# A first feed-forward stage computed as seven block products instead of eight

## The chip, the cores and the metric

The kernel runs on one core of one Trainium2 chip. The metric is the device time of one execution in microseconds, the median of three runs. The engines are called PE (TensorE; PEld is its weight load), DVE (VectorE), ACT (ScalarE), POOL (GpSimd) and SP (SyncE, which here only issues DMAs).

## The reference

```python
# q, k, v: (4, 12, 448, 64) float32; w1, w2, w3, w_out: 768x768; w_in: 768x2048; w_out2: 2048x768
scores = q @ k.transpose(0, 1, 3, 2) / sqrt(64) - log(448)
attn = (1 / (1 + exp(-scores))) @ v                      # a sigmoid, no softmax
x = attn.transpose(0, 2, 1, 3).reshape(1792, 768)
h = maximum(maximum(x @ w1, x @ w2), x @ w3)             # stage b below
y = h @ w_out                                            # stage c
d = y @ w_in                                             # stage d
g = maximum(d, 0) + alpha * minimum(d, 0)
out = g @ w_out2                                         # stage e
```

The weights come as 64-bit floats, all else as 32-bit floats.

## The kernel before

Every matmul has 32-bit operands in a reduced format (fp32r), so each operand is split into a high part `hi` (a cast on ACT) and the rest `lo` (a subtraction on DVE), and a product is three matmuls: lo x hi, hi x lo, hi x hi. Activations are kept transposed: 128 features on the partitions, tokens in the columns. Weights are the stationary operand, loaded in units of 768 rows by 128 columns as two halves of 384; a half arrives as pairs of 32-bit words, ACT and DVE rebuild a 32-bit float of it (`first`, `unit`, `shift`, `sign`, `whole_word`), and then `hi` and `lo` split it. Three raw buffers (`wr`) hold halves; `load_half(z + 3)` is issued on SP's queue behind `whole_word` of half z.

**Attention** works on 24 pairs of heads, two pairs an iteration. For each pair SP loads q and k by 128-byte runs into three buffers each, POOL loads v; DVE turns q and k, casts and subtracts (`prep_ops`); PE computes scores by chunks of 128 keys into three PSUM buffers of two banks (`scores`), one sigmoid on ACT reads 896 columns, and `av` multiplies by v into `pav`. `to_x` casts and subtracts `pav` straight into the x tiles. The 1792 tokens are cut in tiles of 512, 512, 512 and 256, so a batch of 448 straddles two tiles. From pair 12 on, operations that convert the first two weight units are slipped in (`early`).

**Stage b** (`ff1`) takes for each of the six blocks of 128 features of h the units of w1, w2, w3, and for each unit the four token tiles: 6 row blocks x 3 matmuls of 512 columns, or for the short tile 12 matmuls of 512 and 256 with hi and lo side by side. The first result is copied to `mx`, the others are maximized into it on DVE; the third is split into h, which stays in SBUF. **Stage c** is the same over h. **Stages d and e** (`ff2`) alternate in eight steps of two units of w_in (d) and two rows of w_out2 (e); e's sums are kept in SBUF and added to on DVE; the short tile of e swaps its operands (`e_short`).

Nothing is scheduled by a tool: the order of each engine is the order of the program. Conversion work waits in a list (`pending`), of which a fixed number of operations is run after each PSUM group.

Of the kernel before, what the change touches and what calls it, by code (L numbers as in the profile page):

```python
# [16 lines left out]
P = 128  # L17


@with_exitstack  # L20
def kernel(
# [14 lines left out]

# [22 lines left out]
    assert KH == P // 2 and 2 * D == P and (H // 2) % 2 == 0  # L59
# [5 lines left out]
    UN = 768  # L65
    HF = UN // 2
    T = B * S
    TW = 512
    spans = [(c, min(TW, T - c)) for c in range(0, T, TW)]
    NT = len(spans)  # L70
    HW = spans[-1][1]
    assert 2 * HW == TW
# [5 lines left out]
    tpool = ctx.enter_context(tc.tile_pool(name="tpool", bufs=1))  # L78
    xpool = ctx.enter_context(tc.tile_pool(name="xpool", bufs=1))
# [7 lines left out]
    units = []  # L87
    for m in range(KF1):
        for w in (w1, w2, w3):
            units.append((w, "col", m, "w"))  # L90
    for m in range(KDM):
        units.append((w_o1, "col", m, "w"))
    SK = 2
    for s in range(KF2 // SK):
        for f in range(SK):
            units.append((w_in, "col", SK * s + f, "w"))
        for f in range(SK):
            units.append((w_o2, "row", SK * s + f, "e"))
    NU = len(units)

    epool = {}
    wraw, wsp = {}, {}

    def load_half(z):
        u, h = divmod(z, 2)
        if u >= NU:
            return
        w, kind, m, _ = units[u]
        t = wpool.tile([P, HF, 2], U32, tag="wr", name=f"wr{z}", bufs=3)
        if kind == "col":  # L110
            nk = HF // P
            nc.sync.dma_start(
                out=t.rearrange("p (k f) t -> p k (f t)", k=nk),
                in_=w[h * nk * P : (h + 1) * nk * P, 2 * m * P : 2 * (m + 1) * P].rearrange(
                    "(k p) f -> p k f", p=P
                ),
            )
        else:
            nc.sync.dma_start(
                out=t.rearrange("p f t -> p (f t)"),  # L120
                in_=w[m * P : (m + 1) * P, 2 * h * HF : 2 * (h + 1) * HF],
            )
        wraw[z] = t

    def conv_ops(u):

        if u >= NU:
            return []
        tag = units[u][3]
        ops = []  # L130

        def begin():
            pool = epool["e"] if tag == "e" else wpool
            wsp[u] = (
                pool.tile([P, UN], F32R, tag=f"{tag}h", name=f"wh{u}", bufs=2),
                pool.tile([P, UN], F32R, tag=f"{tag}l", name=f"wl{u}", bufs=2),
            )

        for h in range(2):
            z = 2 * u + h  # L140
            st = {}

            def part(i, u=u, h=h):

                if units[u][1] == "col":
                    return wsp[u][i][:, h * HF : (h + 1) * HF]
                return wsp[u][i].rearrange("p (m g j) -> p g m j", m=KDM, g=4)[:, 2 * h : 2 * h + 2]

            def seen(x, u=u):
                x = x.bitcast(F32)  # L150
                return x if units[u][1] == "col" else x.rearrange("p (g m j) -> p g m j", g=2, m=KDM)

            def first(z=z, h=h, st=st):
                if h == 0:
                    begin()
                st["r"] = wraw.pop(z)
                st["T"] = wpool.tile([P, HF], U32, tag="wt", name=f"wt{z}", bufs=3)
                nc.scalar.activation(  # L158
                    st["T"].bitcast(F32),
                    st["r"][:, :, 1].bitcast(F32),  # L160
                    AF.Abs,
                    scale=2.0**-112,
                )

            def unit(st=st):
                nc.scalar.activation(st["r"][:, :, 0], st["r"][:, :, 0], AF.Copy, scale=2.0**-29)  # L166

            def shift(st=st):
                nc.vector.tensor_scalar(st["T"], st["T"], 3, None, ALU.logical_shift_left)

            def sign(st=st):
                nc.vector.scalar_tensor_tensor(  # L172
                    out=st["r"][:, :, 0],
                    in0=st["r"][:, :, 1],
                    scalar=0x80000000,
                    in1=st["r"][:, :, 0],
                    op0=ALU.bitwise_and,
                    op1=ALU.bitwise_or,
                )

            def whole_word(z=z, st=st):
                nc.vector.tensor_tensor(out=st["T"], in0=st["r"][:, :, 0], in1=st["T"], op=ALU.add)  # L182
                load_half(z + 3)

            def hi(st=st, part=part, seen=seen):
                nc.scalar.copy(part(0), seen(st["T"]))  # L186

            def lo(st=st, part=part, seen=seen):
                nc.vector.tensor_sub(part(1), seen(st["T"]), part(0).bitcast(F32))  # L189

            ops += [first, unit, shift, sign, whole_word, hi, lo]
        return ops

    def tmp(nm, t):
        return tpool.tile([P, TW], F32, tag="tmp", name=nm, bufs=5)[:, : spans[t][1]]


    def three(x):
        return x[:, 0], x[:, 1], x.rearrange("p a n -> p (a n)")

    def xy_tile(nm, t):
        if t == NT - 1:
            x = xpool.tile([P, KDM, 2, HW], F32R, tag=f"xyh{t}", name=f"{nm}{t}")
            return [three(x[:, r]) for r in range(KDM)]
        h = xpool.tile([P, KDM, TW], F32R, tag=f"xyh{t}", name=f"{nm}h{t}")
        l = xpool.tile([P, KDM, TW], F32R, tag=f"xyl{t}", name=f"{nm}l{t}")
        return [(h[:, r], l[:, r], None) for r in range(KDM)]


    def attention(apool, ps_s, ps_v):  # L210
# [4 lines left out]
        pairs = [(b, p) for b in range(B) for p in range(NPAIR)]  # L215
# [6 lines left out]
        def load_first():  # L222

            kn = apool.tile([P, NB32, 32], F32, tag="kr", name="kn", bufs=3)
            qn = apool.tile([P, NB32, 32], F32, tag="qr", name="qn", bufs=3)
            for t, src, queue in ((kn, k, nc.sync), (qn, q, nc.scalar)):
                queue.dma_start(
                    out=t.rearrange("p n d -> p (n d)"),
                    in_=src[0, :2].rearrange("j (p n) d -> (j p) (n d)", p=D),
                )  # L230
            raw[0] = (qn, kn)

        def first_pair():

            qn, kn = raw.pop(0)
            for which, t in (("k", kn), ("q", qn)):
# [14 lines left out]
                else:  # L251
                    hi = apool.tile([P, S], F32R, tag="qh", name="qh0", bufs=2)
                    lo = apool.tile([P, S], F32R, tag="ql", name="ql0", bufs=2)
# [22 lines left out]
        def load_pair(i):  # L276
# [3 lines left out]
            qr = apool.tile([P, NB32, 32], F32, tag="qr", name=f"qr{i}", bufs=3)  # L280
            kr = apool.tile([P, NB32, 32], F32, tag="kr", name=f"kr{i}", bufs=3)
# [12 lines left out]
        def prep_ops(i):  # L294
# [6 lines left out]
            def turn(which, src):  # L301
                t = apool.tile([P, S], F32, tag=f"{which}t", name=f"{which}t{i}", bufs=2)
# [9 lines left out]
            def cut(which, copy=nc.vector.tensor_copy):  # L312
# [4 lines left out]
                else:  # L317
                    hi = apool.tile([P, S], F32R, tag="qh", name=f"qh{i}", bufs=2)
                    lo = apool.tile([P, S], F32R, tag="ql", name=f"ql{i}", bufs=2)
# [12 lines left out]
        def scores(i, c, sc=None, stop=True):  # L332
# [20 lines left out]
            if stop:  # L353
                key = (i // 2, "s") if c == NCH else (i, c)
                a = apool.tile([P, 2, S], F32, tag="a", name=f"a{i}_{c}", bufs=2 * NCH + 1)
                at[key] = a
                nc.scalar.activation(a, sc[:, :, :S], AF.Sigmoid, bias=bias_s, scale=scale)  # L357
            return sc

        def av(i, c, start, stop):  # L360
# [5 lines left out]
            for j in range(2):  # L366
# [3 lines left out]
                    a[r, j, :],  # L370
# [17 lines left out]
        def to_x(i):  # L388
            b, p = pairs[i]
            pav = pv.pop(i)  # L390
            parts = []
            for t, (c0, w) in enumerate(spans):
                c, e = max(c0, b * S), min(c0 + w, b * S + S)
                if c < e:
                    if t not in xt:
                        xt[t] = xy_tile("x", t)
                    xh, xl, _ = xt[t][p]
                    parts.append((xh[:, c - c0 : e - c0], xl[:, c - c0 : e - c0], pav[:, c - b * S : e - b * S]))
            for xh, _, ps in parts:
                nc.scalar.copy(xh, ps)  # L400
            for xh, xl, ps in parts:
                nc.vector.tensor_sub(xl, ps, xh.bitcast(F32))
# [4 lines left out]
        zeros = apool.tile([P, TW], BF16, tag="zeros", name="zeros")  # L407
# [23 lines left out]
        early = []  # L431
        for i in range(0, n, 2):
            for z in range(2):
# [32 lines left out]
                for _ in range(3):  # L466
                    if early:
                        early.pop(0)()
# [5 lines left out]
        for f in early:  # L474
            f()
        nc.scalar.activation(nalpha, alpha_sb, AF.Copy, scale=-1.0)

    xt, yt, ht = {}, {}, {}

    def terms(n, wu, col, src):

        hi, lo = wu
# [304 lines left out]
```

## Time and profile before

| | us |
|---|---|
| median of 3 runs (955.95 to 958.16) | 956.27 |
| the profiled execution | 956.26 |
| its span, first to last instruction | 954.5 |
| PE busy | 944.8 |
| DVE busy | 562.1 |
| ACT busy | 408.2 |
| POOL busy | 54.5 |

The profiled execution lies 1.8 us above its span. Busy time of PE includes time in which a matmul waits inside the pipeline. Mean durations of one instruction reach from its start until its writes are acknowledged, so one can start before the one ahead of it on the same engine has ended.

### The profile page before, as it was taken

The numbers are of one execution on the slowest core, as the hardware profiler recorded it, in microseconds if no ns is written. First come the engines' busy times: TensorE is split into PE (matmuls) and PEld (weight loads), VectorE is DVE, ScalarE is ACT, GpSimd is POOL, SyncE is SP. The second block draws the span as 40 slices with busy tenths as digits, with TensorE's granted clock in tenths as the row PEclk, the third lists the DMA queues.
The fourth block names the chain that finished last, engine by engine and source line by source line (L and its number), as shares of the span: only waits on it lengthen the run. The fifth ranks groups of instructions, "written<-read, shape, count | busy, mean of one in ns | idle before, by whom it ended". The sixth has DMA issues, their size and how long they took to land.

```text
span 954.5 us, 12435 instructions
## 1 busy us (share of the span) xinstructions
PE 944.8 (99%) x4730; PEld 752.0 (79%) x4730; DVE 562.1 (59%) x1070; ACT 408.2 (43%) x785; POOL 54.5 (6%) x83
## 2 busy tenths in 40 slices
PE   8999999999999999999999999999999999999997
PEld 5555548888888888888888888888888888888886
DVE  5778752535344454545456368667586775757666
ACT  5777852223232323233357654442525434264320
POOL 4333310000000000000000000000000000000001
PEclk9999999999999999999999999999999999999999
DMA  8999930121121121121121122212122120222016
GB/s 149 145 162 136 157 69 29 39 67 54 47 67 50 50 67 53 46 67 50 50 83 56 62 66 67 67 30 70 35 67 66 49 68 17 67 67 67 17 33 199
DMA packets 132699, 66.88 MB, mean 70 GB/s; under 512 B 91568, under 2 KB 126224, under 8 KB 132640
## 3 DMA queue, kind: packets, MB, share of 16 engines
q1 hardware_dynamic: 127648, 57.60, 25.9%
q0 software_dynamic: 3616, 7.64, 3.2%
q10 hardware_dynamic: 1376, 0.85, 0.3%
q8 instruction: 37, 0.61, 0.3%
q14 instruction: 22, 0.18, 0.1%
HBM read 60.56 MB, written 5.51 MB: 69 GB/s over the span
## 4 chain that ended last, share of the span: by engine, by line
PE 92%; DMA 2%; SPq 2%; DVE 2%; issue 0%; ACT 0%; DVEq 0%
PE b L507 27%; PE d L507 24%; PE e L507 21%; PE c L507 9%; PE pav L367 4%; PE sc L346 4%; PE e_short L675 3%; SPq L286 2%; DMA qr<-in_q_dram 2%; DMA kr<-in_k_dram 0%; DMA kn<-in_k_dram 0%; DVE qt L303 0%; DVE ql L321 0%; DVE wt L182 0%; DVE accs L689 0%
## 5 line engine op out<-in xcount | busy, mean ns | idle before, releaser
L186 ACT CAST wh<-wt 128x384 fp32r<-128x384 f32 x112 | 57.6, 514 | 185.7 <-DVE wt L182 185.6
L507 PE MATMUL b<-xh,wl 128*128 128x512 f32 x324 | 126.3, 390 | 0.0
L507 PE MATMUL b<-xl,wh 128*128 128x512 f32 x324 | 126.1, 389 | 0.0
L507 PE MATMUL d<-yh,wl 128*128 128x512 f32 x288 | 112.2, 390 | 0.0
L507 PE MATMUL d<-yl,wh 128*128 128x512 f32 x288 | 112.2, 390 | 0.0
L654 DVE TENSOR_TENSOR acc<-e,acc 128x512 f32<-128x512 f32 x126 | 85.7, 685 | 18.5 <-PE e L507 18.2
L507 PE MATMUL b<-xh,wh 128*128 128x512 f32 x324 | 91.0, 389 | 0.0
L357 ACT ACTIVATE a<-sc,bias_s 128x896 f32<-128x896 f32 x84 | 79.1, 1010 | 22.1 <-PE sc L346 21.9
L189 DVE TENSOR_TENSOR wl<-wt,wh 128x384 fp32r<-128x384 f32 x112 | 62.1, 555 | 34.5 <-ACT wh L186 34.5
L507 PE MATMUL d<-yh,wh 128*128 128x512 f32 x288 | 80.9, 389 | 0.0
L600 DVE SCALAR_TENSOR_TENSOR r<-n,nalpha,r 128x512 f32<-128x512 f32 (+1 forms) x64 | 43.8, 684 | 55.1 <-ACT n L597 55.0
L507 PEld LDWEIGHTS b<-xh,wl 128*128 128x128 f32 x324 | 60.8, 188 | 13.6 <-issue 0.7
L507 PEld LDWEIGHTS b<-xh,wh 128*128 128x128 f32 x324 | 60.8, 188 | 12.6
L367 PE MATMUL pav<-a,vt 128*64 128x448 f32 (+1 forms) x384 | 70.3, 551 | 0.0
L507 PEld LDWEIGHTS b<-xl,wh 128*128 128x128 f32 x324 | 60.9, 188 | 12.0
L172 DVE SCALAR_TENSOR_TENSOR wr<-wr 128x384 uint32<-128x384 uint32 x112 | 62.3, 556 | 5.4 <-ACT wr L166 2.6
L182 DVE CUSTOM_DVE_ANT_0 wt<-wr,wt 128x768 uint16<-128x768 uint16 x112 | 62.5, 558 | 3.4
L507 PEld LDWEIGHTS d<-yh,wh 128*128 128x128 f32 x288 | 54.1, 188 | 11.3
L507 PEld LDWEIGHTS d<-yh,wl 128*128 128x128 f32 x288 | 54.0, 188 | 11.2
L507 PEld LDWEIGHTS d<-yl,wh 128*128 128x128 f32 x288 | 54.1, 188 | 10.8
L158 ACT ACTIVATE wt<-wr 128x384 f32<-128x384 f32 x112 | 61.7, 551 | 0.0
L166 ACT ACTIVATE wr<-wr 128x384 uint32<-128x384 uint32 x112 | 61.4, 548 | 0.0
(159 smaller groups left out, 1724.2 us busy)
## 6 DMA issues: line engine op xcount, KB each, us to landing
wr<-in_moe_w_out_dram SPq DMA_DIRECT2D x44, 384.0 KB, 3.1
wr<-in_moe_w_dram SPq DMA_DIRECT2D x36, 384.0 KB, 3.3
wr<-in_moe_w_in_dram SPq DMA_DIRECT2D x32, 384.0 KB, 3.2
kr<-in_k_dram SPq DMA_DIRECT2D x92, 56.0 KB, 3.8
qr<-in_q_dram SPq DMA_DIRECT2D x92, 56.0 KB, 3.5
vt<-in_v_dram POOLq DMA_DIRECT2D x46, 96.0 KB, 3.8
out_dram<-o SPq DMA_DIRECT2D x6, 384.0 KB, 4.5
out_dram<-o POOLq DMA_DIRECT2D x6, 384.0 KB, 7.1
```

The source lines that it names most:

```text
L158: nc.scalar.activation(st["T"].bitcast(F32), st["r"][:, :, 1].bitcast(F32), AF.Abs, scale=2.0**-112,)
L166: nc.scalar.activation(st["r"][:, :, 0], st["r"][:, :, 0], AF.Copy, scale=2.0**-29)
L172: nc.vector.scalar_tensor_tensor(out=st["r"][:, :, 0], in0=st["r"][:, :, 1], scalar=0x80000000, in1=st["r"][:, :, 0], op0=ALU.bitwise_and, ...
L182: nc.vector.tensor_tensor(out=st["T"], in0=st["r"][:, :, 0], in1=st["T"], op=ALU.add)
L186: nc.scalar.copy(part(0), seen(st["T"]))
L189: nc.vector.tensor_sub(part(1), seen(st["T"]), part(0).bitcast(F32))
L346: nc.tensor.matmul(sc[:, j, :S], kx[r, c0 : c0 + P], qx[r], start=(start and z == 0), stop=(stop and z == 2),)
L357: nc.scalar.activation(a, sc[:, :, :S], AF.Sigmoid, bias=bias_s, scale=scale)
L367: nc.tensor.matmul(pv[i][j * D : (j + 1) * D, :S], vts[i][r, j, c, :], a[r, j, :], start=start, stop=stop,)
L507: nc.tensor.matmul(ps[:, :w], lt, rh, start=(z == 0), stop=(z == len(mms) - 1))
L600: nc.vector.scalar_tensor_tensor(out=r_, in0=n_, scalar=nalpha[:, m : m + 1], in1=r_, op0=ALU.mult, op1=ALU.add,)
L654: nc.vector.tensor_tensor(out=acc[m, t], in0=ps, in1=acc[m, t], op=ALU.add)
```

## The change

Stage b is computed by a two-by-two block algorithm with seven products (the Strassen-Winograd form). The blocks of a weight matrix are two halves of its rows (384 each) by two neighbouring 128-column units; the blocks of x are the same two halves of features by two tiles of 448 tokens (two batches). Sums and differences of weight blocks are formed from the rebuilt words (`unit_ops`), those of x blocks during attention (`form_ops`), and each of the seven left and seven right operands is split into hi and lo. Partial results are shared: PSUM bank X goes on from product 0 through 3, 4 and 5, with its state copied out after 0 (into bank V, on which product 1 goes on), 3 and 4; bank W takes products 2 and 6.

All tiles become 448 tokens wide and are taken from pools of one-size slots (61, 48, 10 and 24). The sigmoid is two of 448 columns. Pairs of heads come in another order. Of the six blocks of h the first four go to DRAM as they are made (POOL's queue) and are loaded back and split ahead of stage c; the last two stay. The list of pending work is replaced by operations with dependencies and a credit for each engine (`advance`): a step credits so many columns, and an operation costs its columns plus 150. The conversion of the first weights starts at pair 18 instead of 12. Stages c, d and e keep their algorithm, with four equal tiles; the last tile is stored in three parts.

```diff
+    def advance(cols, free=False):
+        now[0] += 1
+        for e in credit:
+            credit[e] = min(credit[e] + cols, cols if e == "D" else 2 * cols // 3)
+        for todo in (urgent, flow):
...
+                if (
+                    (free or o.engine == "Q" or credit[o.engine] > 0)
+                    and all(d.step is not None and d.step < now[0] for d in o.deps)
+                    and (o.gate is None or o.gate())
+                ):
+                    o.fn()
...
+    def split_ops(dst, nm, src, pool, w, *deps, seen=lambda x: x, put=lambda x: x, **kw):
+
+        def hi():
+            dst[0] = slot(f"{nm}h", pool, w, F32R)
+            nc.scalar.copy(put(dst[0]), seen(src()))
+
+        def lo():
+            dst[1] = slot(f"{nm}l", pool, w, F32R)
+            nc.vector.tensor_sub(put(dst[1]), seen(src()), put(dst[0]).bitcast(F32))
...
+        w0 = word_ops(z)
+        l0 = cut(0, lambda: word[z], w0)
+        w1 = word_ops(z + 1)
+        l1 = cut(1, lambda: word[z + 1], w1)
+        w2, w3 = word_ops(z + 2), word_ops(z + 3)
+        o1 = op("D", HF, sum1, w2, w3)
+        cut(2, lambda: t["s"], o1)
+        o3 = op("D", HF, sum3, o1, w0)
+        o2 = op("D", HF, sum2, o1, o3, l0)
+        cut(3, lambda: word[z], o2)
+        cut(4, lambda: word[z + 2], o3)
+        cut(5, lambda: word[z + 3], w3)
+        cut(6, lambda: word[z + 1], op("D", HF, sum4, l1, o2))
...
+        if n == 0:
+            cut(0, B11)
+        elif n == 1:
+            cut(1, B21)
+        elif n == 2:
+            fdone[B11, "t1"] = op("D", TW, t1)
+            cut(2, T1, fdone[B11, "t1"])
+        else:
+            o3 = op("D", TW, t3, fdone[B11, "t1"])
+            o2 = op("D", TW, t2, fdone[B11, 2])
+            cut(3, T1, o2)
+            cut(4, B12, o3)
+            cut(5, B21, op("D", TW, t4, o2, fdone[B11, 1]))
+            cut(6, B22)
...
-                a = apool.tile([P, 2, S], F32, tag="a", name=f"a{i}_{c}", bufs=2 * NCH + 1)
-                at[key] = a
-                nc.scalar.activation(a, sc[:, :, :S], AF.Sigmoid, bias=bias_s, scale=scale)
+                at[key] = [slot(f"a{i}_{c}_{j}") for j in range(2)]
+                for j in range(2):
+                    nc.scalar.activation(at[key][j], sc[:, j, :S], AF.Sigmoid, bias=bias_s, scale=scale)
...
+            x32[i] = slot(f"x{i}")
+            nc.scalar.copy(x32[i], pv.pop(i)[:, :S])
+            form_ops(i)
...
-                if i + z == 12:
-                    early = conv_ops(0) + conv_ops(1)
+                if i + z == 18:
+                    unit_ops(0)
                 ops = prep_ops(i + z + 1)
 
                 def prep():
                     if ops:
                         ops.pop(0)()
+                    advance(650)
...
+                if u < NU - 1:
+                    hd[m, t] = dpool.tile([P, TW], F32, tag=f"h{m}_{t}", name=f"hd{m}_{t}")
+                    nc.gpsimd.dma_start(out=hd[m, t], in_=c)
+                else:
+                    ht[m, t] = {}
+                    split_ops(ht[m, t], f"h{m}_{t}", lambda: c, "b", TW, soon=True)
...
+            if k == 0:
+                banks[X] = bank(ps_m, nm + "X")
+                group(banks[X], mms, stop=False)
+                banks[V] = bank(ps_m, nm + "V")
+                nc.scalar.copy(banks[V][:, :TW], banks[X][:, :TW])
+                spend("A", TW)
+            elif k == 1:
+                group(banks[V], mms, start=False)
+                evict(u, g, 0, 0, banks.pop(V)[:, :TW])
+            elif k == 2:
+                banks[W] = bank(ps_m, nm + "W")
+                group(banks[W], mms, stop=False)
+            elif k in (3, 4):
+                group(banks[X], mms, start=False, stop=False)
+                side[g, k] = slot(f"u{u}_{g}_{k}")
+                nc.scalar.copy(side[g, k], banks[X][:, :TW])
+                spend("A", TW)
+                if k == 4:
+                    evict(u, g, 1, 1, banks[W][:, :TW], side.pop((g, 4)))
+            elif k == 5:
+                group(banks[X], mms, start=False)
+                evict(u, g, 1, 0, banks.pop(X)[:, :TW])
+            else:
+                group(banks[W], mms, start=False)
+                evict(u, g, 0, 1, banks.pop(W)[:, :TW], side.pop((g, 3)))
...
+        order += [(u, k, g) for u in range(1, L) for k in range(7) for g in range(2) if (u, k) > (1, 1)]
+        order += [(L, k, g) for k, g in (
+            (0, 0), (0, 1), (1, 0), (2, 0), (1, 1), (3, 0), (2, 1), (4, 0), (3, 1), (5, 0), (4, 1),
+            (6, 0), (5, 1),
+        )]
+        order += [(0, 0), (L, 6, 1), (0, 1), (1, 0), (1, 1), (0, 2), (0, 3), (1, 2), (1, 3)]
+        order += [(m, t) for m in range(2, KDM) for t in range(NT)]
...
+                    for m, t in ((m, t) for t in range(2, 4) for m in range(KDM - 2)):
+                        reload(m, t, (L, 5 if t == 2 else 6, 1), (L, 6, 1))
+            product(*x)
+            advance(STEP)
```

The order lists products (unit, product, token group) and, with two numbers, stage c's groups (feature block, tile). `STEP` is 1700 columns; a c or d group gives two steps.

## Rows read from the trace of the kernel before

**Rows 1.** The page's first part: busy us (share of span) and instructions.

```profile
PE 944.8 (99%) x4730; PEld 752.0 (79%) x4730; DVE 562.1 (59%) x1070; ACT 408.2 (43%) x785; POOL 54.5 (6%) x83
```

**Rows 2.** Chain of work that ended last: start us, us, what, instructions.

```profile
52.19 3.32 PE pav L367 x20
...
63.24 3.34 PE pav L367 x20
...
143.57 258.70 PE b L507 x1188
402.27 86.16 PE c L507 x396
...
517.15 24.49 PE e L507 x108
541.63 4.24 PE e_short L675 x24
...
939.75 4.31 PE d L507 x36
...
946.95 2.15 DVE accs L689 x4
```

**Rows 3.** Busy time by engine in two stretches of attention.

```profile
core 0: us, PE busy (x) PEld busy (x) DVE busy (x) ACT busy (x) POOL busy (x), PEclk, DMA share, GB/s
85.00:96.00 11.00, 11.00 (x82) 6.11 (x80) 9.21 (x21) 8.54 (x14) 4.35 (x6) 1.00 1.07 160
107.00:118.00 11.00, 11.00 (x84) 6.06 (x82) 8.57 (x20) 8.87 (x15) 4.28 (x6) 1.00 1.03 161
```

**Rows 4.** Groups by line and shape, ACT: busy us, mean ns; idle before.

```profile
L357 ACT ACTIVATE a<-sc,bias_s 128x896 f32<-128x896 f32 x84 | 79.1, 1010 | 22.1 <-PE sc L346 21.9
...
L186 ACT CAST wh<-wt 128x384 fp32r<-128x384 f32 x112 | 57.6, 514 | 185.7 <-DVE wt L182 185.6
...
L606 ACT CAST g_0h<-r 128x512 fp32r<-128x512 f32 x16 | 9.9, 622 | 8.9 <-DVE r L600 8.9
...
L400 ACT CAST xh<-pav 128x448 fp32r<-128x448 f32 x6 | 3.3, 542 | 3.7 <-PE pav L367 3.7
```

**Rows 5.** The same view, DVE.

```profile
L182 DVE CUSTOM_DVE_ANT_0 wt<-wr,wt 128x768 uint16<-128x768 uint16 x112 | 62.5, 558 | 3.4
L172 DVE SCALAR_TENSOR_TENSOR wr<-wr 128x384 uint32<-128x384 uint32 x112 | 62.3, 556 | 5.4 <-ACT wr L166 2.6
L189 DVE TENSOR_TENSOR wl<-wt,wh 128x384 fp32r<-128x384 f32 x112 | 62.1, 555 | 34.5 <-ACT wh L186 34.5
...
L169 DVE TENSOR_SCALAR wt<-wt 128x384 uint32<-128x384 uint32 x112 | 39.8, 355 | 15.4 <-ACT wt L158 14.8
...
L559 DVE TENSOR_TENSOR mx<-b,mx 128x512 f32<-128x512 f32 x36 | 24.9, 692 | 56.1 <-PE b L507 56.1
...
L303 DVE STREAM_TRANSPOSE qt<-qr 128x448 f32<-128x448 f32 x23 | 14.7, 641 | 4.7 <-DMA qr<-in_q_dram 4.6
...
L321 DVE TENSOR_TENSOR kl<-kt,kh 128x448 fp32r<-128x448 f32 x23 | 14.4, 626 | 0.8
...
L320 DVE CAST kh<-kt 128x448 fp32r<-128x448 f32 x23 | 9.1, 394 | 2.7 <-DVE kt L303 0.5
```

**Rows 6.** Timeline of one iteration: start us, us of the merged piece.

```profile
84.20 2.81 ACT L357 ACTIVATE a<-sc,bias_s 128x896 f32<-128x896 f32 x3 [0.25 <-PE sc L346]
```

**Rows 7.** The page's DMA issues: count, KB each, us to landing.

```profile
vt<-in_v_dram POOLq DMA_DIRECT2D x46, 96.0 KB, 3.8
...
out_dram<-o POOLq DMA_DIRECT2D x6, 384.0 KB, 7.1
```

**Rows 8.** Waits from 20 to 140 us: total us, times, longest us.

```profile
DVE xl L402 <- ACT xh L400: 12.1, 14, 2.3
...
PEld sc L346 <- ACT a L357: 7.2, 9, 1.6
```

More of the change, by code (lines that the diff above doesn't have):

```diff
@@ L64 @@
     KF2 = DF2 // P
[L65 to L72, printed above, removed]
+    HK = KDM // 2
+    HF = HK * P
+    TW = S
+    NT = B
+    assert KDM == KF1 and NPAIR == KDM
     scale = 1.0 / math.sqrt(D)
@@ L118, in load_half @@
         else:
+            c = 2 * 32 * HK
             nc.sync.dma_start(
-                out=t.rearrange("p f t -> p (f t)"),
-                in_=w[m * P : (m + 1) * P, 2 * h * HF : 2 * (h + 1) * HF],
-            )
[L123 to L136, printed above, removed]
-            )
[L139 to L192, printed above, removed]
@@ L210, in attention, with __init__ @@
-    def attention(apool, ps_s, ps_v):
-        pairs = [(b, p) for b in range(B) for p in range(NPAIR)]
+                out=t.rearrange("p (g f) t -> p g (f t)", g=4),
+                in_=w[m * P : (m + 1) * P].rearrange("p (g f) -> p g f", g=4)[
+                    :, :, h * c : (h + 1) * c
+                ],
+            )
+        wraw[z], since[z] = t, now[0]
+    class Op:
+        def __init__(self, engine, cols, fn, deps, gate):
+            self.engine, self.cols, self.fn, self.deps, self.gate = engine, cols + 150, fn, deps, gate
+            self.step = None
@@ new lines, with op @@
+    urgent, flow = [], []
+    credit = {"A": 0, "D": 0}
+    def op(engine, cols, fn, *deps, gate=None, soon=False):
+        o = Op(engine, cols, fn, [d for d in deps if d is not None], gate)
+        (urgent if soon else flow).append(o)
+        return o
+    def advance(cols, free=False):
[3 more added lines that the diff above has]
+        for todo in (urgent, flow):
+            n = 0
+            while n < len(todo):
+                o = todo[n]
+                if (
[4 more added lines that the diff above has]
+                    o.fn()
+                    o.step = now[0]
+                    if o.engine != "Q":
+                        credit[o.engine] -= o.cols
+                    todo.pop(n)
+                else:
+                    n += 1
@@ new lines, in weight, with terms, group @@
+    def weight(z, r):
+        f = wsp[z + r // HK]
+        return tuple(f[x][:, r % HK * P : (r % HK + 1) * P] for x in range(2))
+    def terms(pairs):
+        got, late = [], []
+        for lt, rt in pairs[:-1]:
+            a, b = three(lt, rt)
+            got += a
+            late += b
+        a, b = three(*pairs[-1])
+        return got + late + a + b
+    def group(ps, mms, start=True, stop=True):
+        for z, (lt, rh) in enumerate(mms):
+            nc.tensor.matmul(
+                ps[:, :TW], lt, rh, start=(start and z == 0), stop=(stop and z == len(mms) - 1),
+                skip_group_check=True,
+            )
@@ L738 @@
-    with tc.manual_schedule():
+                drain()
+                more.close()
+                opool = ctx.enter_context(
+                    tc.tile_pool(name="turned", bufs=1, side="right", reuse_waits="tile")
+                )
+                for t in range(NT):
+                    for f in range(SK):
+                        d_group(s, f, t)
+                    if t:
+                        e_tile(s, t - 1)
+                e_tile(s, NT - 1)
+        assert not flow and not urgent
```

583 lines of the change are left out of this document (311 added, 272 removed).

## The prediction

> **What bounds the kernel now.** I read the page's engine line first, then the chain of work that ended last in order of time, then busy time by stretch. PE is busy for nearly the whole span while DVE, ACT and POOL have room [rows 1]. But a busy PE may be waiting inside a matmul, so the chain decides: from 143.57 us it is PE alone, one stage after the other without a gap, until 946.95 us, and then 7.5 us of accumulation and store [rows 2]. So 803.4 us of the 954.5 us span are a matmul stream, and what it costs is matmuls times their spacing.
>
> The spacing is read from the same pieces [rows 2]: 108 matmuls of 512 columns in 24.49 us are 226.8 ns each, 36 of 256 columns in 4.31 us are 119.7 ns. That is 0.4184 ns a column (the 2.4 GHz level; the granted clock is 1.00 [rows 3]) and 12.6 ns for each matmul whatever its width. A matmul of 448 columns, which the trace lacks with a full 128x128 weight, then costs 12.6 + 448 x 0.4184 = 200.0 ns. The 384-column group is the check on that line: 24 in 4.24 us are 176.7 ns against 173.3 by the line, so a weight load does not set the pace there.
>
> Ahead of 143.57 us is attention. Two pairs of heads take 63.24 - 52.19 = 11.05 us, again at PE's pace [rows 2]; in 11 us DVE is then busy for 8.6 to 9.2 us, ACT for 8.5 to 8.9, and the DMA share is 1.03 to 1.07 [rows 3]. Four resources are nearly full there, and only there.
>
> **The matmul stream.** Before, the b stage is 18 weight units of 66 matmuls, 1188. After, it is 9 units (a pair of 128-column blocks of one matrix) x 7 products x 2 token groups x 9 matmuls (3 row blocks x 3 hi/lo terms) = 1134, all 448 wide: 226.8 us in place of 258.70 [rows 2], 31.9 less. Stage c becomes 6 x 4 x 18 = 432 matmuls, 86.4 us for 86.16. Stages d and e become 1152 each; 2304 x 200.0 = 460.8 us for 803.4 - 258.7 - 86.2 = 458.5. Their columns do not change: four tiles of 448 merely need more matmuls than three of 512 and a packed short one. In all 3870 x 200.0 = 774.0 us against 803.4: **-29.4 us**. Each ns of error in the 200.0 is 3.9 us.
>
> The Trainium skill, page "TensorE: Matmul & The Clock Gate", section "Back-to-back issue gap", gives a warm gap of columns over 2.4 GHz plus about 2.5 ns: 189.2 ns for 448 columns, and the stream would be an estimated 732 us. The trace disagrees where it can be asked: by that rule 512 columns are 215.8 ns, and the chain shows 226.8. I go by the rows.
>
> **Attention.** PE's matmuls are the same. ACT: each of the 84 sigmoids of 896 becomes two of 448. Three of them in a row take 2.81 us with a last one of 1.01 [rows 4, 6], so one is started each 0.90 us; one of 448 costs between half of that, 0.45, and the 0.542 us of a 448-column copy out of PSUM [rows 4]. An iteration of two pairs then has 14 sigmoids, 6.3 to 7.6 us, two copies of x, 1.1, and 3.5 hi casts (7 cuts for four pairs; 0.57 us each, between 514 ns for 384 and 622 for 512 columns [rows 4]), 2.0: 9.4 to 10.7 us of 11.05. DVE has for each pair two transposes, two casts, two subtractions (2 x (0.641 + 0.394 + 0.626) = 3.32 us [rows 5]) and 11 operations for four pairs (7 lo, 4 sums; 0.626 each), 1.72: 10.1 us of 11.05 an iteration. In the last three iterations the first unit's weights come on top: four halves at 0.355 + 0.556 + 0.558 and 11 operations at 0.555 [rows 5], 12.0 us on DVE. The credit admits 650 for each of 8 steps, about 8.7 operations of 598 and 5.4 us, so an iteration has at most 6.64 + 5.4 = 12.0 us on DVE, 1.0 over; three give 3.0. What is not admitted is left for the b stage, whose first four products (7.2 us) need none of the second token group. SP: the halves' loads move from pair 12 to 18, each behind the DVE whole-word operation three halves earlier, with q and k loads queued after them; q and k now take slots from a shared pool of 61 in place of three buffers, which lets SP run ahead. A stall of 1.6 us, PE held by a sigmoid [rows 8], may go. I take **+3 us**, from -1.6 (it only goes) to +26: lo waited on hi for 12.1 us in 14 waits, 0.9 each [rows 8], and 3.5 such waits an iteration on top of 10.1 us of work overrun 11.05 by 2.2, 26 in twelve. I stay near the low end, since a lo is now issued at least one step after its hi.
>
> **The b stage off PE.** DVE for one unit (14 products, 25.2 us): four halves 5.9, four sums and seven lo 6.1, and for each token group up to six reads of PSUM at no more than the 0.692 us of the 512-column max [rows 5], 8.3: 20.3 us. ACT: less than that. Neither is full. New on PE's path: a second product cannot continue a bank before ACT has copied it (k=1 on V; 4 and 5 on X), 3 waits x 18 = 54; behind such a copy on ACT stand the next unit's weight operations, with a whole unit of slack. The cover is the other token group's product, 9 x 0.2 = 1.8 us, against 0.542 for the copy and a hand-off that I estimate at 0.3 from the 0.25 us that ACT idled before PE's bank reached it [rows 6]. Cost between nothing and 54 x 0.9 = 49 us were the cover gone. I take **+1.5**, for the order of the first and last unit and for leftover operations.
>
> **h through DRAM.** 16 tiles of 224 KB go out and come back on POOL's queue, which after the v loads holds nothing else until the output. A landing takes 3.8 us for 96 KB and 7.1 for 384 KB [rows 7], so about 5. Writing has at least a whole unit of time. Reading back for tiles 2 and 3 is issued as the last b products are, 16 us (the last product and four c groups at 3.6 us) before c first needs it; eight casts and subtractions, about 5 us on each engine, fit. **+1 us**, from 0 to 8 if queue, slots and splits add up. The end (add, transpose, store) stays near its 7.5 us.
>
> Sum: 956.26 (the profiled execution; the median is 956.27) - 29.4 + 3 + 1.5 + 1 = **932 us**.
>
> **Rivals.**
> (a) Attention becomes bound by DVE and ACT waiting on each other, +8 to +26 us: 937 to 955. For it: both at 85 to 97% by the sums above. Against: DVE was at 9.2 of 11 with no gap on PE [rows 3]. Chance 0.20.
> (b) Slower than before: PE waits for ACT's bank copies. The place is the start of each product that continues a bank; decisive once the 54 waits average above 29.4 / 54 = 0.54 us, that is when ACT answers more than 1.5 us late. At the full 0.9 us it is 956.3 - 29.4 + 49, some 976. Against: ACT has half of each unit free. Chance 0.06.
> (c) The h tiles or their splits reach c late, +5 to +8: 936 to 940. Chance 0.06.
> (d) The change does not pay because 448 columns cost more than the line says. Attention's 64-row matmuls of 448 come in pairs, so give no price; if a shorter matmul left 7 ns of weight load bare, 3870 x 7 = 27 us: 959. Against: 256 columns pass at 119.7 ns. Chance 0.03.
> (e) The fixed 12.6 ns vanishes at 448: 3870 x 187.4 = 725 us, the time 883. Against: it is there at 256 as at 512 columns. The skill's rule named above points this way. Chance 0.01.
>
> **How the numbers follow.** The forecast, 0.64, has its own range of 925 to 940. To leave out no more than 2 in 10 I reach into (a): 924 to 950, which holds the forecast, (c) and most of (a). This kernel can tell 0.3%, 2.9 us, from no change. Faster by more: forecast, (c), (e) and most of (a), 0.89. Within: the end of (a) and some of (d), 0.04. Slower: (b) and the rest, 0.07.
>
> **What would show it.** The chain should be PE alone from about 147 us on, with b's 1134 matmuls in 227 to 230 us and c, d, e at 200 ns a matmul. DVE and ACT in attention should be busy for 9.5 to 11 us of 11, and an iteration stay near 11 us until the last three. Waits of PE on ACT copies in b should be short or none. Wrong if: iterations of attention grow from the first on (a), PE idles before every continued product (b), or at c's third tile (c), or the spacing is not 200 ns (d, e).

## The result and the profile after

The changed kernel took 944.65 us (median of 4, 943.07 to 945.38) against 956.59 (955.95 to 958.16) on the same chip: ratio 0.9871, 95% interval 0.9853 to 0.9888. That is 1.3% faster, half of the forecast gain (932), and inside the range. The profiled execution took 944.47 us, 1.9 more than its span. A later set of twelve executions gave 944.43, with a few near 955, of which experiment 8 tells more.

The engine line, and the chain of work that ended last in order of time (start, us, what), both of the changed kernel:

```profile
PE 925.7 (98%) x4892; PEld 802.7 (85%) x4892; DVE 612.2 (65%) x1175; ACT 453.3 (48%) x932; POOL 74.0 (8%) x119
```

```profile
54.35 3.32 PE pav L468 x20
...
147.33 2.02 PE b_0X L587 x9
...
375.59 3.65 PE c L587 x18
381.06 83.91 PE c L587 x414
464.97 29.18 PE d L587 x144
494.15 29.18 PE e L587 x144
...
910.02 7.31 PE d L587 x36
```

The chain has the forecast shape: PE alone from 147.33 us, b in 228 us, c entered without a wait. But 29.18 / 144 is 202.7 ns a matmul, not 200.0, in every stage. Setting the ends beside those of [rows 2] gives where the 11.9 us of span came from. The last matmul ends at 948.51 us before and at 931.91 after, by the timelines (start, us, engine, line, what; before, then after):

```profile
947.99 0.52 PE L675 MATMUL e_short<-wh,g 128*128 128x384 f32 x2
```

```profile
931.54 0.37 PE L587 MATMUL e<-g_3h,w111h 128*128 128x448 f32 x1
```

| | before | after | change | forecast |
|---|---|---|---|---|
| start of the first b matmul | 143.57 | 147.33 | +3.8 | +3 |
| from there to the end of the last matmul | 804.9 | 784.6 | -20.4 | -29.4 + 2.5 of waits |
| from there to the end of the span | 6.0 | 10.7 | +4.7 | 0 |

Busy time by stretch in late attention (stretch, its length, PE, PEld, DVE, ACT, POOL with counts, granted clock, DMA share, GB/s), to be set beside [rows 3]:

```profile
87.50:98.50 11.00, 11.00 (x84) 6.05 (x84) 9.81 (x19) 10.28 (x21) 4.29 (x6) 1.00 1.05 141
109.60:120.60 11.00, 10.68 (x74) 5.37 (x74) 10.00 (x21) 11.00 (x24) 4.24 (x6) 1.00 0.67 121
120.60:131.60 11.00, 10.37 (x70) 5.05 (x72) 9.98 (x22) 11.00 (x24) 4.25 (x6) 1.00 1.03 180
```

Through most of attention PE stays full with DVE at 9.8 and ACT at 10.3 of 11. Once the first unit's weights are slipped in, it is ACT that has no moment left (11.00 of 11), and the chain runs through its sigmoids; the two iterations there take 12.1 and 12.0 us in place of 11.05. (In the last iteration, from 134.6 to 138.0 us, the chain runs through DVE.) The chain, in those iterations and at its beginning:

```profile
10.81 5.27 DMA qr<-in_q_dram
17.42 3.29 PE sc L447 x18
...
30.22 2.04 PE sc L447 x18
...
117.75 1.06 ACT a L458 x2
...
119.72 0.96 ACT a L458 x2
```

A stretch there, with the granted clock third from the end:

```profile
18.00:22.00 4.00, 4.00 (x24) 2.22 (x22) 2.26 (x4) 3.52 (x7) 0.00 (x0) 0.57 0.76 100
```

Up to 17.42 us PE waits 1.5 us for that q load and for DVE's work on it, and behind the wait the granted clock is 0.5 (the 1.2 GHz level) from 18.3 to 21.7 us: 18 matmuls take 3.29 us in place of 2.04. From there to 109 us attention is 2.2 us behind the kernel before (54.35 us in the chain above, 52.19 in [rows 2]); the weights add the other 1.6. The loss at the beginning differs between executions: in four of the profiles with the same attention b starts at 145.3 to 145.7 us, in the other five at 146.8 to 147.8.

What ACT waits for in b, in the list of waits (us in total, times, longest), and what h's trip through DRAM costs, in the list of DMA issues (count, KB each, median us to landing):

```profile
ACT b_0V L645 <- PE b_0X L587: 41.9, 9, 7.3
ACT u L656 <- PE b_0X L587: 37.4, 16, 6.1
```

```profile
hr<-hd POOLq DMA_DIRECT2D x16, 224.0 KB, 5.5
```

In b, ACT waits for PE, not PE for ACT; a tile of h comes back in 5.5 us, close to the 5 estimated (on the way out it lands in 2.2), and c's chain has no gap.

### The profile page after: what moved, and what is told of

The parts are those of the page before. It is cut to its first block, busy times and chain, and to the rows that moved or that the text cites. A ratio compares the mean times of both kernels' runs of the same rounds, so it can differ in the third digit from the quotient of the medians.

```text
span 942.6 us, 13100 instructions
## 1 busy us (share of the span) xinstructions
PE 925.7 (98%) x4892; PEld 802.7 (85%) x4892; DVE 612.2 (65%) x1175; ACT 453.3 (48%) x932; POOL 74.0 (8%) x119
## 4 chain that ended last, share of the span: by engine, by line
PE 94%; DVE 2%; ACT 1%; DMA 1%; SPq 1%; issue 0%; POOL 0%; POOLq 0%; ACTq 0%; DVEq 0%
PE d L587 25%; PE e L587 23%; PE c L587 9%; PE b_0X L587 7%; PE b_1X L587 7%; PE pav L468 6%; PE sc L447 6%; PE b_0W L587 3%; PE b_1W L587 3%; PE b_0V L587 2%; PE b_1V L587 2%; ACT a L458 1%; DVE o L809 1%; DVE acc L806 1%; SPq L388 1%; DMA qr<-in_q_dram 1%
## 5 line engine op out<-in xcount | busy, mean ns | idle before, releaser
L806 DVE TENSOR_TENSOR acc<-e,acc 128x448 f32<-128x448 f32 x168 | 101.7, 617 | 36.4 <-PE e L587 34.1
L752 DVE SCALAR_TENSOR_TENSOR r<-n,nalpha,r 128x448 f32<-128x448 f32 x64 | 43.7, 684 | 105.0 <-ACT n L749 104.7
L748 ACT ACTIVATE r<-d 128x448 f32<-128x448 f32 x64 | 34.9, 545 | 156.8 <-PE d L587 156.8
L458 ACT ACTIVATE a<-sc,bias_s 128x448 f32<-128x448 f32 x168 | 96.4, 664 | 7.9 <-PE sc L447 7.9
L178 DVE TENSOR_SCALAR wt<-wt 128x384 uint32<-128x384 uint32 x112 | 39.7, 354 | 10.1 <-ACT wt L172 10.1
L447 PE MATMUL sc<-qh,kh 64*128 64x448 f32 x192 | 38.7, 399 | 4.2 <-DVE qh L421 2.6
L369 POOL DMA_DIRECT2D vt<-in_v_dram x46 | 35.4, 772 | 68.6 <-PE pav L468 68.6
L447 PE MATMUL sc<-ql,kh 64*128 64x448 f32 x192 | 36.2, 373 | 0.0
L447 PE MATMUL sc<-qh,kl 64*128 64x448 f32 x192 | 35.8, 368 | 0.0
L749 ACT ACTIVATE n<-d 128x448 f32<-128x448 f32 x64 | 34.5, 540 | 0.0
```

Of the source, the lines that this page charges most:

```text
L369: queue.dma_start(out=vt[:, j, :NCH], in_=v[b, 2 * p + j, k0 : k0 + NCH * P].rearrange("(c p) d -> p c d", p=P),)
L447: nc.tensor.matmul(sc[:, j, :S], kx[r, c0 : c0 + P], qx[r], start=(start and z == 0), stop=(stop and z == 2),)
L458: nc.scalar.activation(at[key][j], sc[:, j, :S], AF.Sigmoid, bias=bias_s, scale=scale)
L752: nc.vector.scalar_tensor_tensor(out=st["r"], in0=st["n"], scalar=nalpha[:, m : m + 1], in1=st["r"], op0=ALU.mult, op1=ALU.add,)
L806: nc.vector.tensor_tensor(out=a, in0=ps[:, :TW], in1=a, op=ALU.add)
```

## Experiments

Each is an edit of the changed kernel unless said otherwise; E stands for one execution.

**1 and 2. Is 202.7 ns the price of the width?** Two kernels that step the width of the matmuls: the changed kernel by stages (widths_slots), and the kernel before, in its 512-token tiles (widths_tiles).

```diff
-    def group(ps, mms, start=True, stop=True):
+    def group(ps, mms, start=True, stop=True, w=TW):
         for z, (lt, rh) in enumerate(mms):
+            n = w if z else TW
             nc.tensor.matmul(
-                ps[:, :TW], lt, rh, start=...
+                ps[:, :n], lt, rh[:, :n], start=...
...
+                w=(448, 440, 432, 424, 416, 408, 400, 392)[s],
...
+                group(ps, mms, w=(384, 376, 368, 352, 336, 320, 288, 256)[s])
```

> The changed kernel, in which all matmuls of a group but the first stream fewer columns: in c 448 to 412 by feature block, in d 448 to 392 and in e 384 to 256 by step; it leaves out the rest of those columns, so only the spacing of its matmuls is read. Theory A (the cost above the column time is not fixed but depends on the width): 256 columns stay near 120 ns, 384 near 176.7, 448 at 202.7, and the excess over the line 12.6 + 0.4184 ns a column rises and falls in between. Theory B (the cost is fixed, but matmuls on tiles in 1792-byte slots pay 2.7 ns more): every width lies the same 2.7 ns above the line, 256 columns at 122.4 and 384 at 176.0.

> The kernel before, in which all matmuls of a group on a 512-column tile but the first stream fewer columns: 448 to 412 in c, 504 to 400 and 448 in d, 508 to 256 in e; it leaves out the rest, so only the spacing is read. Theory A (width decides): 448 columns cost 202.7 ns here too, in tiles that start at multiples of 2048 bytes. Theory B (the slots decide): 448 columns cost the 200.0 ns of the line, and so do all others lie on the line.

Mean spacing in ns from start to start, worked out from the two traces, beside the prediction's line 12.6 + 0.4184 a column:

```
columns        256   320   352   384   400   416   432   448   464   480   488   496   504   512
widths_slots 121.7 146.0 159.8 175.0 180.4 188.6 195.9 202.7     -     -     -     -     -     -
widths_tiles 119.7 147.2 160.9 176.2 180.7 188.3 195.6 203.1 209.5 217.0 225.8 220.0 227.2 227.0
line         119.7 146.5 159.9 173.3 180.0 186.7 193.3 200.0 206.7 213.4 216.8 220.1 223.5 226.8
```

At 448 the two kernels agree within 0.5 ns, so neither the slots nor the changed layout makes the 202.7: that width costs it in either kernel. (The mean at 256 in widths_slots holds two stray gaps of 222 and 196, most are 117 to 120; that in widths_tiles leaves one of 223 out.) The line holds at 256 and within 1 ns at 320, 352, 400, 496 and 512. It fails in between, by 1.6 to 3.6 ns at the other widths from 384 to 480 by 3.7 at 504 and by 9.0 at 488, which costs more than the wider 496. Its two ends were good points, and 448 is a bad one. The width does not say all: in stage c at 436 columns the means are 196.8 in widths_slots and 193.4 in widths_tiles. What makes these steps no run here shows.

**3. The four equal tiles alone (tiles448).** The kernel before with 448-token tiles, the eight products kept:

```diff
-    TW = 512
+    TW = 448
...
-                for t in range(NT - 1):
+                for t in range(NT):
...
-                e_short(s, range(SK))
```

> One part alone: the kernel before with four equal token tiles of 448 in all stages in place of 512, 512, 512 and 256, eight block products' worth of work as before, no slots, no trip through DRAM. 4032 matmuls. Theory A and theory B (this kernel's tiles start at multiples of 1792 bytes too) both give 202.7 ns each, 817 us from the first b matmul to the last of e in place of 803.4: some 970 us with an unchanged end, a few more as the whole last tile is stored after the last matmul. The line of the prediction gives 200.0 ns, 806.4 us, and 959 us plus that store.

973.91 us (973.23 to 974.64), ratio 1.0184 (1.0167 to 1.0201). Its chain, with 1296 and 432 matmuls for b and c:

```profile
143.11 262.86 PE b L502 x1296
405.97 87.55 PE c L502 x432
493.52 29.19 PE d L502 x144
```

262.86 / 1296 is 202.8 ns. So the tiles cost some 17.6 us (973.91 against 956.32 for the kernel before in the same set), and the rest of the change, the seven products above all, brings back 29.3 (973.91 to 944.65), close to the 162 matmuls that b saves (32.8) less the later entry of b (143.11 to 147.33, 4.2). The tail of this kernel is 11.2 us: it comes with the tiles.

**4 and 5. When the first weights are converted.** unit12 begins at pair 12 instead of 18, unit22 at pair 22:

```diff
-                if i + z == 18:
+                if i + z == 12:
```

> The changed kernel with the conversion of the first weight unit begun at pair 12 instead of 18. Theory C (the last three iterations of attention are late because ACT, busy for 11.0 us of 11 there, has the weights on top): ACT's load spreads over six iterations with about 1 us of room each, the first b matmul comes 1 to 2 us earlier, and the time is 943. Rival D (ACT has no room in the iterations before either; each grows by what is moved in): the first b matmul stays or comes later, and the time is 944 to 947.

> The changed kernel with the conversion of the first weight unit begun at pair 22 instead of 18. Theory D (attention's iterations grow by what the weights put on ACT, wherever they are put): iterations stay at 11.05 us until pair 22, the late ones of 12.1 and 12.4 us go, and what is not converted stalls the first products of b by several us. Rival G (the operand cuts of x alone overfill ACT and DVE in the last iterations): they stay at 12 us.

unit12 took 945.54 us (10 E, 943.58 to 956.32; ratio 0.9914, 0.9879 to 0.9949): nothing gained. Its first b matmul starts at 146.99 us although its beginning is undisturbed, 1.3 to 1.7 us later than in the four such profiles above, and the longer iterations lie earlier; ACT is as full there, and later DVE. Stretches of unit12, and two pieces of its chain:

```profile
83.00:96.00 13.00, 11.69 (x82) 5.93 (x80) 10.53 (x23) 12.45 (x26) 4.25 (x6) 1.00 1.00 190
120.00:132.00 12.00, 12.00 (x86) 6.26 (x84) 11.83 (x24) 11.89 (x25) 4.25 (x6) 1.00 0.79 117
```

```profile
86.24 4.18 DMA qr<-in_q_dram
...
95.15 4.76 DMA kr<-in_k_dram
```

So ACT is not alone there: the chain also waits for loads of q and k, which stand in SP's queue behind the weights' loads. How much each of them costs is not separated.

unit22 took 954.69 us (1 E), with 202.7 ns a matmul to its end. Its late attention iterations stay at 11.05 us and b starts at 143.35, 2 us ahead of the changed kernel where its beginning is undisturbed (145.3): that much of its +3.8 is the weights. But then b lacks its operands. Its chain in time, and a stretch of it:

```profile
143.35 2.04 PE b_0X L587 x9
145.46 0.52 ACT b_0V L645
145.98 0.43 ACT f_1h L198
...
154.80 3.73 PE b_0W L587 x9
```

```profile
149.00:159.00 10.00, 4.20 (x11) 3.78 (x12) 9.93 (x21) 4.54 (x10) 0.00 (x0) 0.50 0.31 82
```

PE waits three times in the first 40 us of b, for 9.6, 1.8 and 0.6 us. During the first of these waits the granted clock falls to 0.5 (the 1.2 GHz level), from 149.0 to 159.2 us, and the matmuls behind it are 373 ns apart, some 2 us more; together it is 14 us. Work for the first unit costs time at each of the three places tried; 18 is near the best of them.

**6. The cover of the bank copies (one_group).** Six of the nine units do one token group's seven products in sequence, so that products 1, 4 and 5 of each follow the product whose bank ACT has to copy with nothing between (36 in all):

```diff
-        order += [(u, k, g) for u in range(1, L) for k in range(7) for g in range(2) if (u, k) > (1, 1)]
+        order += [(1, k, g) for k in range(2, 7) for g in range(2)]
+        order += [(u, k, g) for u in range(2, L) for g in range(2) for k in range(7)]
```

> The changed kernel with the seven products of one token group one after the other in six of the nine units, so that a product that continues a bank follows its predecessor at once and ACT's copy of the bank has no cover: 36 such products. By the prediction's 0.9 us for an uncovered copy and hand-off it is 32 us slower, some 977. The rival: the hand-off is cheaper than estimated, at 0.54 us for the copy alone 20 us, some 964; if the copies are hidden anyway, 945.

986.03 us (1 E). Its chain around two such products:

```profile
203.06 1.84 PE b_0X L587 x9
...
204.93 0.54 ACT u L656
...
205.51 2.13 PE b_0X L587 x9
...
207.66 0.54 ACT u L656
...
208.25 2.09 PE b_0X L587 x9
```

Two such products start 2.74 us apart (205.51 and 208.25) in place of 1.82: 0.9 us each, the price of rival (b), and 36 of them are the 32 us of stalls that this run has in b. The cover that the change's order gives is what keeps b free of it. A second thing showed: from 401.5 us on the matmuls of this run are 206.7 ns apart, not 202.7, through all of c, d and e, another 11 us. And within b each stretch of matmuls behind a wait of PE has one spacing to its end: of the 25 stretches of 25 matmuls or more that begin at such a wait 19 settle at 202.7 and 6 at 206.7, among them the last one, which reaches to the end of the run.

**7. The tail: which store is late.** tail_queues moves the last tile's middle part from SP's queue to ACT's; tail_two stores it in two parts instead of three, on SP's and ACT's queues alone; tail_early in four:

```diff
-                (other if g % 2 else nc.sync).dma_start(
+                first = nc.scalar if t == NT - 1 and h1 == KDM - 1 else nc.sync
+                (other if g % 2 else first).dma_start(
```

```diff
-                    if t == NT - 1 and m + 1 in (HK, KDM - 1):
-                        store(t, o, 0 if m < HK else HK, m + 1)
+                    if t == NT - 1 and m in (1, 3, 4):
+                        store(t, o, {1: 0, 3: 2, 4: 4}[m], m + 1)
```

> The changed kernel with the two stores of the last tile's middle part that SP issues given to ACT. Theory E (SP's queue holds the end: eight stores one after the other from 926.8 to 938.3 us, each of the last ones 1.3 to 1.5 us): SP's last issue comes some 2.7 us earlier, the last landing 2 to 3 us earlier, the time is 942. Rival F (the short runs themselves hold it, whichever queue issues them): ACT's issues take as long, the last landing stays near 7.3 us behind the last transpose, the time is 944.5.

> The changed kernel with its last tile stored in two parts (five blocks, then the last) in place of three, on SP and ACT: 8 stores in place of 12. Theory E: SP issues six in place of eight and the last landing comes 2 to 3 us earlier, 942. Rival F (short runs): a third fewer runs, and the first part starts 2.4 us later than the first of three did; the end stays or moves less than 1 us.

945.42 us (10 E, ratio 0.9921, 0.9882 to 0.9959) and 945.49 us (10 E, 0.9912, 0.9872 to 0.9952): no gain. The last landing comes 10.0 and 9.9 us after the start of the last matmul, in the changed kernel 9.6. A fourth kernel leaves out the first half of the last tile's stores, 0.69 MB:

> The changed kernel, with the first half (384 of 768 columns) of the last tile's output never stored, so 0.69 MB less goes out in the last 15 us; the other two parts of that tile are stored as before. In the changed kernel the last landing comes 9.6 us after the start of the last matmul (931.5 to 941.2 us), and the DMA share stays near 1 until 940 us. Theory H: the end waits for bytes that were issued earlier and still stand in line, so without the first half the last landing comes 2 to 5 us earlier, 5 to 7.5 us after the last matmul's start. Rival: the last part of 128-byte runs sets the end by itself (add, transpose, issue, landing in some 6 us); then the distance stays 9 us or more.

> The changed kernel, with the last tile stored in four parts as they are made (columns of feature blocks 0-1, 2-3, 4, 5) in place of three (0-2, 3-4, 5). Theory H: the same bytes, of which a third can leave 3.6 us sooner, so the last landing comes 1 to 2 us earlier and the time is some 943 us, unless shorter runs (256 bytes in place of 384) cost what the earlier start gives, then 944.5. Rival (the last part sets the end by itself): no change, 944.5 us, with the last landing still 9.6 us after the start of the last matmul.

The end of the changed kernel, and then that of tail_less, by stretch (DMA share and GB/s stand last):

```profile
932.00:934.00 2.00, 0.00 (x0) 0.00 (x0) 1.80 (x4) 0.00 (x0) 0.85 (x2) 1.00 0.99 283
934.00:936.00 2.00, 0.00 (x0) 0.00 (x0) 0.00 (x0) 0.00 (x0) 0.41 (x1) 1.00 1.00 250
936.00:938.00 2.00, 0.00 (x0) 0.00 (x0) 0.00 (x0) 0.00 (x0) 0.00 (x0) 0.63 0.94 184
938.00:940.00 2.00, 0.00 (x0) 0.00 (x0) 0.00 (x0) 0.00 (x0) 0.00 (x0) 0.50 0.87 136
```

```profile
930.00:932.00 2.00, 0.14 (x1) 0.00 (x0) 1.93 (x4) 0.00 (x0) 0.78 (x2) 1.00 0.66 220
932.00:934.00 2.00, 0.00 (x0) 0.00 (x0) 0.10 (x1) 0.00 (x0) 0.47 (x1) 0.56 0.90 164
934.00:936.00 2.00, 0.00 (x0) 0.00 (x0) 0.00 (x0) 0.00 (x0) 0.00 (x0) 0.50 0.84 138
936.00:938.00 2.00, 0.00 (x0) 0.00 (x0) 0.00 (x0) 0.00 (x0) 0.00 (x0) 0.50 0.16 29
```

In the changed kernel the DMA engines are busy for 0.87 of the time or more for 8 us after PE has ended, at a rate that falls as the parts get narrower. (Part of the early rate is POOL's: of the 0.57 MB between 932 and 934 us its queue moved 0.44, in packets of up to 4608 bytes.) Without the first half the last landing comes 7.2 us after the last matmul's start, 2.4 sooner. That run also has four stores fewer, but so has tail_two with all the bytes, and it ends as late as before. So, by these runs, the end waits for bytes in line, not for the queue that issues them.

tail_early gained nothing either: 945.71 us (10 E, 0.9901, 0.9876 to 0.9926), its last landing 10.9 us after the last matmul's start. But it is no test of an earlier start. In the list of SP's waits there is a new one, for a store to land:

```profile
SPq L780 <- DMA out_dram<-o: 2.5, 1, 2.5
```

Behind this wait SP issues its last two stores at 949.27 and 949.64 us, 6.5 us after the last transpose has ended, and the share of the DMA engines falls from 0.91 (946 to 948 us) to 0.39 (950 to 952).

**8. Two lengths.** Of the 40 executions of unit12, tail_queues, tail_two and tail_early 27 took 942 to 947 us and 13 took 954 to 958. The profile of tail_early fell on a long one: 202.7 ns until 368 us, 206.7 ns to the end. The place where it changes is the only one between the start of b and the end where PE is held. ACT's work and PE's weight load there, in the timeline of the changed kernel (start, us, engine, line, what, idle time before and its releaser):

```profile
368.33 0.57 ACT L198 CAST h_1h<-mx 128x448 fp32r<-128x448 f32 x1 [1.35 <-DVE mx L223]
368.81 0.56 ACT L198 CAST h_1h<-hr 128x448 fp32r<-128x448 f32 x1
369.28 0.52 ACT L656 COPY u<-b_1X 128x448 f32<-128x448 f32 x1
...
369.85 0.19 PEld L587 LDWEIGHTS b_1X<-x_0h,f_4l 128*128 128x128 f32 x1 [0.17 <-ACT u L656]
```

In the last unit, a copy of bank X that PE needs stands on ACT behind a cast that waits 1.35 us for DVE, and PE starts some 0.06 us late. This is the waiting of rival (b), once in 54. The change of spacing in one_group lies behind the same product. I ran the changed kernel again, and a version (no_hold) in which those casts are issued behind the copy:

```diff
-                    split_ops(ht[m, t], f"h{m}_{t}", lambda: c, "b", TW, soon=True)
+                    split_ops(ht[m, t], f"h{m}_{t}", lambda: c, "b", TW, soon=True, gate=lambda: (L, 3, 1) in made or (i, t) != (1, 1))
...
-                        reload(m, t, (L, 3 * t, 0), (L, 2 + 2 * t, 0))
+                        reload(m, t, (L, 3 * t, 0), (L, 3, 1) if t else (L, 2, 0))
```

> The changed kernel itself once more. Of the 40 timed executions of unit12, tail_queues, tail_two and tail_early, which leave b to e as they are, 27 took 942.5 to 946.6 us and 13 took 954.1 to 958.1, none lay between; the four of the changed kernel took 943.1 to 945.4. The profile of tail_early is of one of the long ones (954.73 us): its matmuls are 202.7 ns apart until 368 us and 206.7 ns from there to the end, 2700 x 4.0 = 10.8 us. The change of spacing comes right behind the one place where PE is held between the start of b and the end, for some 0.06 us: product 4 of the second token group in the last unit starts late because ACT's copy of bank X after product 3 stands behind a cast of h that waits for DVE. Theory P (that hold can tip the spacing into its slower pattern, which then lasts as long as PE is never held again): the changed kernel has the same two times, about a third of its executions near 955 and the rest near 944.6. Rival Q (the long times belong to the edited kernels alone): all executions within 943 to 946.5.

> The changed kernel, with that hold taken away: in the last unit ACT's copy of bank X after product 3 of the second group is issued ahead of the casts of h that wait for DVE, and those casts are issued a step later. Nothing else is moved. Theory P: no matmul in b, c, d or e starts late, the spacing stays at 202.7 ns to the end, and all executions are near 944.5 us, none near 955. Rival R (the two times have another cause and the hold is a coincidence): again about a third of the executions near 955. Of about ten executions none would lie near 955 by chance under R with 2 in 100.

The changed kernel itself has both lengths: of 12 E eight took 942.2 to 945.3 us, one 948.5, and three 954.7 to 956.0 (ratio over all 0.9889, 0.9859 to 0.9919). Its profiled execution is a long one; the wait and the chain:

```profile
PEld b_1X L587 <- ACT u L656: 0.2, 1, 0.2
```

```profile
172.62 3.65 PE b_1X L587 x18
375.24 3.72 PE c L587 x18
380.82 85.56 PE c L587 x414
466.38 29.76 PE d L587 x144
```

29.76 / 144 is 206.7 ns, and single gaps there are 206, 207, 207, where the short execution has 199, 202, 203, 203 and 207 in turn. The same 18 matmuls take 3.65 us at 172 and 3.72 at 375 us: the spacing changed in the matmuls right behind that wait (369.4 us in this run). no_hold has no such wait; its chain keeps the shorter spacing:

```profile
381.00 83.91 PE c L587 x414
464.91 29.18 PE d L587 x144
```

It took 943.94 us (4 E, 942.66 to 944.92; ratio 0.9860, 0.9845 to 0.9876), like the changed kernel's short executions. That a held PE can tip the spacing is shown by three profiles at this place (tail_early, after_again, one_group) and by the stretches of one_group's b; the hold alone does not decide it, since seven more profiles (after, unit12, unit22, tail_queues, tail_two, tail_less, widths_slots) have the same hold and stay at 202.7. That no_hold has no long executions rests on four. With 16 long in 56 of the others four short ones would come by chance with (40/56)^4 = 0.26, and with more if the long ones come in clusters, as they may: the three of the changed kernel are among the first four of its twelve. Whether the hold is behind all of the long executions, and what settles the spacing, stays open.

## Why the prediction was right, and where it was off

**The stream.** The mechanism and the counts held: 3870 matmuls, PE alone, -20.4 us. The step that was mis-sized is "12.6 + 448 x 0.4184 = 200.0 ns": it measured 202.7, and 3870 x 2.7 is 10.4 us, most of the 12 us between forecast and result. (That -20.4 is better than -29.4 + 10.4 comes of the reading: the stream before was taken to end at 946.95 us, where the chain passes to DVE, but its last matmul ends at 948.51.) The line was drawn through 256 and 512, both on it, and the one check, 384 at 176.7 for 173.3, was read as "a weight load does not set the pace" when it said that widths between may lie some ns above. The rule cited there (the Trainium skill, "TensorE: Matmul & The Clock Gate", "Back-to-back issue gap") gives 189.2 ns for this width; the trace disagrees, by 13.5 ns. The Trainium skill gives it there as the gap of an isolated matmul. Rival (d), given 0.03 with 7 ns, was right that 448 columns cost more than the line, at less than half its size (experiments 1 and 2), but not that the change does not pay. The reason it gave, a bare weight load, is not shown: the widths 320 and 352 are narrower still and lie within 1 ns of the line.

**Attention.** +3.8 for +3, some 2 of it by a start that the prediction had not in its sum. The iterations stay at 11.05 until the first unit's weights come, as forecast, and rival (a) did not come. But the engine was named wrongly. The sum put the first unit's weights on DVE alone, up to 12.0 us an iteration, and gave them no time on ACT; DVE stood at 10.0 of 11, and ACT, at 9.4 to 10.7 an iteration without these weights, is the one at 11.00. The two sigmoids of 448 have a price of their own: where ACT is full, a pair of them takes 0.96 to 1.06 us in the chain, against 0.90 for one of 896 [rows 6], some 0.1 us for each of 84.

**b off PE's path, and h.** +1.5 and +1 were forecast; the waits are 0.06 us and none. The cover of 1.8 us was right, and one_group puts the price of a bare copy at 0.9 us, as worked out. h's tiles came in time (5.5 us a landing on the way back), so rival (c) did not come. What the prediction did not know is that a single short hold can cost 10.8 us behind it.

**The tail.** "stays near its 7.5 us" was wrong by 3 to 5 us (10.7 from the last matmul's end for 6.0). Before, the last tile held 256 tokens and 0.79 MB, and its stores went out in packets of 1536 bytes; now it holds 448 and 1.38 MB, SP's and ACT's packets of it are 384, 256 and 128 bytes, and the same DMA engines must move them at the end. Taking bytes away shortens the end (tail_less); what the short packets cost by themselves is not separated.

**The range.** 924 to 950 held the median; three of the changed kernel's 16 executions lie above it, at the time of before.

## What to carry to other kernels

Measure the spacing of a matmul at the very width that the kernel will use: a line through two other widths was off by 1.3%, which ate a third of the saving. Price an algorithm and the tiling that it needs apart: here the tiles cost 17.6 us and the rest of the change brought 29.3. By the traces d and e on the old tiles (804.9 - 258.7 - 86.2 = 460.0 us, against 2304 x 202.7 = 467.0 after) would save an estimated 7 more, which was not tried. When a stage is one unbroken stream, look for the one short wait in it before judging a few per cent, since what follows may run at another spacing.

## What the runs showed of the hardware

- The spacing of these matmuls is not one line in the width: on the line at 400 (180.4 ns), 3 ns above it at 448 (202.7), 3.6 at 480 (217.0) and 9 at 488 (225.8), on it again at 496 (220.0) and 512 (227.0), all at a granted clock of 1.00.
- At 448 columns it has two steady values, 202.7 and 206.7 ns, at the same clock. In these profiles it changed only right behind a wait of PE for ACT, in one_group both ways, and in after_again it then stayed for 570 us of unbroken work. What in PE or its queues decides is open.
- While the last tile was stored, busy DMA engines moved ever less: 283 GB/s at a share of 0.99, then 136 at 0.87 when most packets had 128 bytes.
